# Attention and a squared-ReLU MLP on one core: q and k of four head pairs loaded by rows and turned on TensorE

## The chip, the cores and the metric

One core of one Trainium2 chip runs the kernel. The metric is device time in microseconds, the median of several executions; less is better.

## The reference

```python
# q, k, v: (4, 12, 448, 64) float32; w_in (768, 2048) and w_out (2048, 768), given as 8-byte floats
scores = (q @ k.T) / 8                      # for each of 48 heads, causal mask
attn   = softmax(scores)                    # rows of 448
x      = (attn @ v) -> (1792, 768)          # heads side by side
out    = relu(x @ w_in) ** 2 @ w_out        # float32, (1792, 768)
```

## The kernel before

The 48 heads are worked as 24 pairs. Twelve pairs (`NA = 12`, numbered n = 0 to 11, batches 0 and 1) make up the first stage; the other twelve are spread over the MLP of the first half of the rows. The fifth to the eighth pair are n = 4 to 7. Even pairs use one set of buffers (names beginning with a: `ak`, `aq`, `akt`, `aqt`, `ap`, `apt`), odd pairs another (`bk`, `bq`, ...).

For the scores TensorE wants q and k with the 64 dimensions of each head on the partitions (128 for a pair) and the 448 positions along the free dimension. `load_qk` (L350) gets there in two steps: four DMAs for q and four for k of each pair, each 448 pieces of 128 bytes (32 floats), put 32x32 blocks side by side, and `transposed` (L369) turns the blocks with one VectorE instruction for each of q and k.

A pair then goes: scores on TensorE (L388), row minimum with mask on VectorE (L401), exponential on ScalarE (L405), normalisation on GpSimd or VectorE (L414, L416), 16 TensorE transposes of the probabilities in four groups of four (L428), each group copied out of PSUM by ScalarE or VectorE (L312 or L436), the product with v on TensorE (L448), and two instructions that leave x as a high and a low part (L312, L315).

The weights come as 8-byte floats in pieces of 128 rows (L589, `words`), which ScalarE (twice L312), VectorE (L597, L315, L600) and GpSimd (L325, L319) turn into two 4-byte parts. The first MLP product (L636, L637, L638: three matmuls for each step) fills TensorE between the pairs as soon as x and the weight piece of a step exist; two PSUM banks are set aside for it.

A planner in the kernel sets the order of all work. Each step is given a rank, the engines that could do it with a cost, and what it reads and writes; `emit` places the steps one after the other in a model of the engines' times and writes each engine's instructions in that order. A step with two ways (for instance copying a group out of PSUM on ScalarE or VectorE) gets the one whose modelled end, plus a bias of 0.5 for ScalarE and 1.0 for VectorE, comes first. All DMAs that matter here are issued by SyncE (SP) in one queue, in the planner's order, 0.5 us each in its model. Each engine runs its instructions strictly in order.

PSUM has eight banks; the planner lets up to two at a time hold turned blocks (kind `pt`), four scores, one the product with v, two the MLP.

Of the kernel before, what the change touches and what calls it, by code (L numbers as in the profile page):

```python
# [9 lines left out]
F32 = mybir.dt.float32  # L10
# [7 lines left out]
PE, ACT, DVE, POOL, DMA, DMA2 = range(6)  # L18
# [143 lines left out]
def t_act(n, psum=False, more=0):  # L162
    return n / 1200 + (0.17 if psum else 0.215) + 0.15 * more


def t_dve(n, fast=False):
    return n / 1920 + 0.15 if fast else n / 960 + 0.15
# [13 lines left out]
def t_dma(count, size):  # L181
    return count * (0.0084 + size * 0.0000488) / 16
# [3 lines left out]
def kernel(  # L186
# [17 lines left out]
    nc = tc.nc  # L204
    B, H, S, D = q.shape
    DM = out.shape[1]
    DFF = w_in.shape[1]
    P = 128
    QC = P // 2
    NQ = S // QC  # L210
    NK = -(-S // P)
# [26 lines left out]
    PCW = max(GF * P, CH)  # L238
    NRAW, NZ, NB, NR = 3, 3, 1, 6
    HWAY, OWAY, GWAY = slice(None), slice(1, 2), slice(0, 1)  # L240
    TURNS, LEAD = (0, 3, 2, 1), 15
    CB = NP // 2
    CBW = CB * P
# [17 lines left out]
    plan = Plan()  # L261

    def tiles(nm, n, shape, dtype, pool=const):
        return [pool.tile(shape, dtype, name=f"{nm}{i}") for i in range(n)]

    early = ExitStack()
    pool = early.enter_context(tc.tile_pool(name="early", bufs=1, side="right"))
    ident = pool.tile([P, 3 * QC], F32, name="ident")
# [33 lines left out]
    for i in range(2):  # L302
        m = mask[i * QC:(i + 1) * QC, S - QC:]
        nc.gpsimd.affine_select(
            out=m, in_=m, pattern=[[-1, QC]], base=0,
# [5 lines left out]
    def on_act(n, dst, src, psum=False, func=AF.Copy, more=0, **kw):  # L311
        return (ACT, t_act(n, psum, more), lambda: nc.scalar.activation(dst(), src(), func, **kw))  # L312
# [25 lines left out]
    def attention(s, n, at):  # L338

        b, hp = divmod(n, NP)  # L340
        nm = s.nm
        spare = (lambda us: us) if n >= NA else (lambda us: 0.0)

        def load_qk(key, src, t, j):


            queue, eng = (DMA2, nc.scalar) if n < 2 and key == "q" else (DMA, nc.sync)
            for h in range(D // SQ):
                i = (j * D + h * SQ)
                plan.op(at - 14, [(queue, 0.5, lambda h=h, i=i: eng.dma_start(  # L350
                    out=t[i:i + SQ].rearrange("p (b d) -> p b d", d=SQ),
                    in_=src[b, 2 * hp + j, :, h * SQ:(h + 1) * SQ].rearrange(
                        "(b p) d -> p b d", p=SQ),
                ), t_dma(S, 128))], [], [(nm, key, j, h)])

        def load_v():
# [3 lines left out]
            for kc in range(NK):  # L360
                def go(kc=kc, rows=min(P, S - kc * P)):
# [3 lines left out]
                plan.op(at + V_AT[min(n, 2)] + V_STEP * kc, [(DMA, 0.5, go, t_dma(2 * NV * min(P, S - kc * P), 256))],  # L365
                        [], [(hold, kc)], [taken])

        def transposed(key, src, dst, at):
            plan.op(at, [(DVE, t_dve(S), lambda: nc.vector.transpose(dst, src))],  # L369
                    [(nm, key, j, h) for j in range(2) for h in range(D // SQ)], [(nm, key + "t")])  # L370
# [82 lines left out]
                    [(vr, kc) for kc in range(NK)] + [(nm, "pt", i) for i in range(len(TURNED) // 4)], [av], take=av, drop=[vr],  # L453
                    lag=spare(1.0))

        for j in range(2):
            load_qk("k", k, s.k, j)
        for j in range(2):
            load_qk("q", q, s.q, j)
        if n % NV == 0:  # L460
            load_v()
        vr = vs[n // NV]
        transposed("k", s.k, s.kt, at)
        transposed("q", s.q, s.qt, at + 1)
        at += 4
        groups = (ORDER[:3], ORDER[3:]) if n < NA else (ORDER,)
        for chunks in groups:
# [16 lines left out]
        if n < NA:  # L484
            x = x_t[n]
# [592 lines left out]
    PAIR = 8.6  # L1078
    H_US, O_US = 3 * t_mm(S), 3 * t_mm(CH)
    stack, middle = ExitStack(), ExitStack()  # L1080
    odd = Buffers("b", stack.enter_context(tc.tile_pool(name="b", bufs=1)))
    for n in range(NA):
        attention((even, odd)[n % 2], n, n * PAIR)
    start = NA * PAIR + 4
# [42 lines left out]
    for i, n in enumerate(turns):  # L1127
        attention(even, n, start + i * (rank - start - 42) / NA)
# [76 lines left out]
```

## Time and profile before

| | us |
|---|---|
| median of three runs | 612.62 |
| the three runs | 611.44, 612.62, 615.09 |
| the profiled execution: device time | 611.87 |
| its span, first to last instruction | 610.1 |
| TensorE busy, share of the span | 591.2, 97% |
| VectorE, ScalarE, GpSimd busy | 447.0, 357.6, 350.7 |
| mean granted TensorE clock | 0.996 |

The profiled execution is 0.75 us under the median of the runs; 1.8 us of its time lie outside the span. The busy time of TensorE is partly modelled, since its matmuls are pipelined: a busy stretch may still hold gaps.

### The profile page before, as it was taken

What the parts mean: (1) busy time and instruction counts of PE and PEld (TensorE: products, weight loads), DVE (VectorE), ACT (ScalarE), POOL (GpSimd) and SP (SyncE); (2) the same over time, 40 slices, a digit from 0 to 9 for tenths busy, and PEclk for the clock granted to TensorE, in tenths of its full rate; (3) what the DMA queues carried; (4) which work ended last, traced back from release to release, by engine and by line L of the source; (5) the groups of instructions that cost most, each with busy time, mean ns of one, the idle gap of its engine ahead of it and who ended that gap; (6) DMA issues with size and microseconds to landing.
All of it is one profiled execution on the core that took longest, in us unless ns stands there. A gap on an engine that the chain in (4) does not pass through costs nothing.

```text
span 610.1 us, 11412 instructions
## 1 busy us (share of the span) xinstructions
PE 591.2 (97%) x3718; PEld 510.7 (84%) x3718; DVE 447.0 (73%) x961; ACT 357.6 (59%) x880; POOL 350.7 (57%) x459
## 2 busy tenths in 40 slices
PE   3989999999999999999999999999999999999997
PEld 1656677889988988888898889989989999999996
DVE  4988984476886898674887326769996688779764
ACT  3889997766786745677455542256665743652400
POOL 2465773556669756877744864225894666575100
PEclk9998999999999999999999999999999999999999
DMA  9888973598888998999998477867877847863555
GB/s 143 174 178 143 187 175 57 126 311 275 233 239 264 291 241 222 263 280 269 243 266 283 155 197 221 287 198 199 203 142 175 207 123 145 192 144 64 170 91 91
DMA packets 201788, 120.01 MB, mean 197 GB/s; under 512 B 137152, under 2 KB 189696, under 8 KB 201728
## 3 DMA queue, kind: packets, MB, share of 16 engines
q1 hardware_dynamic: 180624, 107.99, 64.9%
q0 software_dynamic: 6912, 9.44, 10.3%
q10 hardware_dynamic: 14192, 1.85, 1.9%
q8 instruction: 29, 0.48, 0.3%
q14 instruction: 31, 0.25, 0.1%
HBM read 80.71 MB, written 38.54 MB: 195 GB/s over the span
## 4 chain that ended last, share of the span: by engine, by line
PE 84%; DMA 5%; DVE 4%; ACT 3%; issue 1%; SPq 1%; POOL 1%; DVEq 0%; ACTq 0%
PE ps L636 7%; PE ps L1055 7%; PE ps L1057 6%; PE ps L1056 6%; PE ps L448 6%; PE ps L638 6%; PE ps L637 6%; PE ps L388 6%; PE ps L428 6%; PE ps L943 5%; PE ps L945 5%; PE ps L944 5%; PE ps L821 4%; PE ps L819 4%; PE ps L817 4%; DMA words<-in_moe_w_in_dram 1%
## 5 line engine op out<-in xcount | busy, mean ns | idle before, releaser
L414 POOL TENSOR_SCALAR ap<-ap,asm 128x128 f32<-128x128 f32 (+6 forms) x122 | 73.7, 623 | 52.6 <-DVE asm L473 41.9
L312 ACT ACTIVATE words<-words 128x384 f32<-128x384 f32 (+3 forms) x131 | 75.1, 598 | 25.7 <-DVE words L315 9.0
L401 DVE CUSTOM_DVE_ANT_0 ps<-ps,mask 128x448 f32<-128x448 f32 (+6 forms) x168 | 68.6, 444 | 22.9 <-PE ps L388 15.0
L1055 PE MATMUL ps<-wo,g 128*128 128x384 f32 x224 | 77.0, 344 | 0.0
L1057 PE MATMUL ps<-wo,g 128*128 128x384 f32 x224 | 75.1, 335 | 0.0
L1056 PE MATMUL ps<-wo,g 128*128 128x384 f32 x224 | 75.0, 335 | 0.0
L636 PE MATMUL ps<-x,wi 128*128 128x448 f32 x192 | 74.7, 389 | 0.0
L638 PE MATMUL ps<-x,wi 128*128 128x448 f32 x192 | 70.4, 367 | 0.4 <-DVE wi L315 0.4
L637 PE MATMUL ps<-x,wi 128*128 128x448 f32 x192 | 70.2, 366 | 0.0
L405 ACT ACTIVATE ap<-ps,mx 128x448 f32<-128x448 f32 (+6 forms) x126 | 58.8, 483 | 15.6 <-DVE mx L401 15.1
L319 POOL TENSOR_TENSOR wi<-words,wi 128x384 fp32r<-128x384 f32 (+1 forms) x47 | 60.3, 1308 | 8.5 <-ACT wi L312 6.9
L325 POOL TENSOR_SCALAR wi<-words 128x384 fp32r<-128x384 f32 (+1 forms) x46 | 31.3, 682 | 56.4 <-DVE words L600 13.3
L312 ACT ACTIVATE r<-ps 128x448 f32<-128x448 f32 x59 | 32.0, 544 | 43.4 <-PE ps L638 14.8
L817 PE MATMUL ps<-x,wi 128*128 128x448 f32 x153 | 56.3, 368 | 0.0
L821 PE MATMUL ps<-x,wi 128*128 128x448 f32 x153 | 56.0, 366 | 0.0
L819 PE MATMUL ps<-x,wi 128*128 128x448 f32 x153 | 56.0, 366 | 0.0
L943 PE MATMUL ps<-g,wi 128*128 128x448 f32 x150 | 55.0, 367 | 0.3 <-ACT sa L312 0.3
L945 PE MATMUL ps<-g,wi 128*128 128x448 f32 x150 | 54.9, 366 | 0.0
L944 PE MATMUL ps<-g,wi 128*128 128x448 f32 x150 | 54.8, 366 | 0.0
L597 DVE TENSOR_SCALAR words<-words 128x384 int32<-128x384 int32 (+1 forms) x56 | 31.9, 573 | 25.3 <-ACT words L312 19.2
L315 DVE CUSTOM_DVE_ANT_0 words<-words 128x768 uint16<-128x768 uint16 (+1 forms) x56 | 44.2, 789 | 6.7 <-ACT words L312 3.2
L312 ACT ACTIVATE apt<-ps 128x512 f32<-128x512 f32 x71 | 39.2, 605 | 16.7 <-PE ps L428 16.5
(144 smaller groups left out, 1487.3 us busy)
## 6 DMA issues: line engine op xcount, KB each, us to landing
words<-in_moe_w_in_dram SPq DMA_DIRECT2D x24, 512.0 KB, 5.2
words<-in_moe_w_out_dram SPq DMA_DIRECT2D x32, 384.0 KB, 4.3
wo_split<-wo SPq DMA_DIRECT2D x26, 384.0 KB, 4.5
wi<-wo_split SPq DMA_DIRECT2D x21, 384.0 KB, 4.0
wo_whole<-words SPq DMA_DIRECT2D x32, 192.0 KB, 3.9
wi_split<-wi SPq DMA_DIRECT2D x24, 256.0 KB, 3.7
v<-in_v_dram SPq DMA_DIRECT2D x24, 192.0 KB, 4.4
wi_whole<-words SPq DMA_DIRECT2D x18, 256.0 KB, 3.8
```

Of the source, the lines that this page charges most:

```text
L312: return (ACT, t_act(n, psum, more), lambda: nc.scalar.activation(dst(), src(), func, **kw))
L636: nc.tensor.matmul(o, w[:, 0], x[:, 0], start=c == 0, stop=False)
L637: nc.tensor.matmul(o, w[:, 0], x[:, 1], start=False, stop=False)
L638: nc.tensor.matmul(o, w[:, 1], x[:, 0], start=False, stop=c == NP - 1)
L817: nc.tensor.matmul(o, w.t[:, 0, c], x[:, 0], start=begin and c == 0, stop=False, skip_group_check=True)
L819: nc.tensor.matmul(o, w.t[:, 0, c], x[:, 1], start=False, stop=False, skip_group_check=True)
L943: nc.tensor.matmul(o, w.t[:, 0, d], g.t[:, 0], start=start, stop=False, skip_group_check=True)
L944: nc.tensor.matmul(o, w.t[:, 0, d], g.t[:, 1], start=False, stop=False, skip_group_check=True)
L945: nc.tensor.matmul(o, w.t[:, 1, d], g.t[:, 0], start=False, stop=stop, skip_group_check=True)
L1055: nc.tensor.matmul(res(), g[:, 0], w[:, 0], start=f == 0, stop=False)
L1056: nc.tensor.matmul(res(), g[:, 0], w[:, 1], start=False, stop=False)
L1057: nc.tensor.matmul(res(), g[:, 1], w[:, 0], start=False, stop=f == GF - 1)
```

## The change

q and k of pairs 4 to 7 no longer pass through the 32x32 blocks. `load_rows` issues two DMAs for q and two for k, one for each head; partition p gets the four consecutive rows 4p to 4p+3, 256 bytes each, on 112 partitions. `turned_rows` then turns each of q and k with four TensorE transposes (112x128 into 128x112) into one PSUM bank of kind `pt`, and one copy out of PSUM, on ScalarE or VectorE, reads the bank with a step of 112 elements so that the positions come out in order. The rows lie in two new buffers shared by the four pairs in turn, so these loads no longer wait for the readers of `ak`, `aq`, `bk`, `bq`. The other 20 pairs are as they were.

```diff
+    ROWS, RB = range(4, 8), S // NK          # RB = 112, NK = 4
...
+        def load_rows(key, src):
+            t = rows_t[n % len(rows_t)][:, "kq".index(key)]
+            for j in range(2):
+                plan.op(at - 14, [(DMA, 0.5, lambda j=j: nc.sync.dma_start(
+                    out=t.rearrange("p (c x) -> p c x", c=NK)[:, :, j * D:(j + 1) * D],
+                    in_=src[b, 2 * hp + j].rearrange("(p c) d -> p c d", c=NK)),
+                    t_dma(S, 4 * D))], [], [("rows", n % len(rows_t), key, j)])
+
+        def turned_rows(key, dst, at):
+            ps = Hold("ps", "pt")
+            t = rows_t[n % len(rows_t)][:, "kq".index(key)]
+            def go():
+                for c in range(NK):
+                    nc.tensor.transpose(ps.t[:, c * RB:(c + 1) * RB], t[:, c * P:(c + 1) * P], ident[:RB, :RB])
+            def src():
+                return ps.t[:, :S].rearrange("p (c i) -> p i c", c=NK)
+            def to():
+                return dst.rearrange("p (i c) -> p i c", c=NK)
+            plan.op(at, [(PE, NK * 0.109, go)], [("rows", n % len(rows_t), key, j) for j in range(2)], [ps], take=ps, clear=[(nm, key + "t")])
+            plan.op(at, [
+                on_act(S, to, src, True),
+                (DVE, t_dve(S) + 0.05, lambda: nc.vector.tensor_copy(to(), src())),
+            ], [ps], [(nm, key + "t")], drop=[ps])
...
-        for j in range(2):
-            load_qk("k", k, s.k, j)
-        for j in range(2):
-            load_qk("q", q, s.q, j)
+        rows = n in ROWS
+        if rows:
+            load_rows("k", k)
+            load_rows("q", q)
+        else:
+            for j in range(2):
+                load_qk("k", k, s.k, j)
+            for j in range(2):
+                load_qk("q", q, s.q, j)
...
-        transposed("k", s.k, s.kt, at)
-        transposed("q", s.q, s.qt, at + 1)
+        if rows:
+            turned_rows("k", s.kt, at)
+            turned_rows("q", s.qt, at + 1)
+        else:
+            transposed("k", s.k, s.kt, at)
+            transposed("q", s.q, s.qt, at + 1)
...
+    rows_t = tiles("rows", 2, [RB, 2, 2 * NK * D], F32, pool)
```

## Rows read from the trace of the kernel before

**Rows 1.** The page: busy time of TensorE, and TensorE in 40 slices.

```profile
PE 591.2 (97%) x3718; PEld 510.7 (84%) x3718; DVE 447.0 (73%) x961; ACT 357.6 (59%) x880; POOL 350.7 (57%) x459
...
PE   3989999999999999999999999999999999999997
```

**Rows 2.** Stretches: length, busy time (count) by engine, clock, DMA share, GB/s.

```profile
20.62:62.22 41.60, 38.17 (x324) 24.84 (x325) 35.09 (x114) 35.50 (x108) 22.60 (x41) 0.96 0.84 162
...
44.00:50.00 6.00, 5.04 (x34) 2.33 (x36) 3.89 (x14) 5.96 (x19) 2.49 (x5) 0.72 0.96 196
62.22:110.00 47.78, 47.17 (x419) 34.53 (x414) 36.69 (x127) 40.47 (x123) 28.63 (x49) 1.00 0.65 131
```

**Rows 3.** Chain of waits, 16 to 56 us: start, length, what.

```profile
24.58 4.33 DMA words<-in_moe_w_in_dram
...
39.11 4.62 DMA words<-in_moe_w_in_dram
...
44.33 0.58 ACT bpt L312
...
52.48 1.75 PE ps L428 x16
```

**Rows 4.** SyncE's issues in order of time, 19 to 47 us: start, length, what.

```profile
19.22 2.05 SPq L350 DMA_DIRECT2D ak<-in_k_dram  x4
21.37 3.16 SPq L350 DMA_DIRECT2D aq<-in_q_dram  x4
...
33.00 2.87 SPq L350 DMA_DIRECT2D ak<-in_k_dram  x4
35.97 3.04 SPq L350 DMA_DIRECT2D aq<-in_q_dram  x4
...
42.51 3.51 SPq L350 DMA_DIRECT2D bq<-in_q_dram  x4
```

**Rows 5.** Issue times in ns (min/median/max) of two loads, 0 to 110 us, and landing.

```profile
L350 SPq DMA_DIRECT2D bk<-in_k_dram x24: 312/477/1864, 3.3 to 72.8; - x24
...
DMA to landing us min/median/max: 2.1/3.4/5.4
...
L362 SPq DMA_DIRECT2D v<-in_v_dram x20: 379/496/2558, 6.6 to 90.6; - x20
```

**Rows 6.** DMA, 57 to 61 us, only 128-byte packets: packets, and the queue's share.

```profile
DMA packets 2941, 0.36 MB, mean 91 GB/s; under 512 B 2941, under 2 KB 2941, under 8 KB 2941
...
q1 hardware_dynamic: 2941, 0.36, 56.5%
```

**Rows 7.** DMA, 46.6 to 50.9 us, mostly v in 256-byte packets.

```profile
DMA packets 2161, 0.96 MB, mean 224 GB/s; under 512 B 2033, under 2 KB 2033, under 8 KB 2161
...
q1 hardware_dynamic: 2161, 0.96, 97.6%
```

**Rows 8.** TensorE in order of time, 17 to 75 us (idle before, and who ended it).

```profile
40.89 2.25 PE L428 MATMUL ps<-ident,bp 128*128 128x128 f32 x16
44.96 4.01 PE L388 MATMUL ps<-bkt,bqt 64*64 64x448 f32 x28 [1.83 <-ACT bpt L312]
48.90 2.16 PE L448 MATMUL ps<-bpt,v 128*64 128x448 f32 x16
...
54.15 2.23 PE L388 MATMUL ps<-akt,aqt 64*64 64x448 f32 x28
56.31 1.95 PE L448 MATMUL ps<-apt,v 128*64 128x448 f32 x16
```

**Rows 9.** Groups by line and shape, 20.62 to 62.22 us: busy us, mean ns.

```profile
L428 PE MATMUL ps<-ident,bp 128*128 128x128 f32 x48 | 7.2, 279 | 1.1 <-POOL bp L414 0.8
...
L312 ACT ACTIVATE words<-words 128x512 f32<-128x512 f32 x5 | 3.5, 700 | 3.6 <-DMA words<-in_moe_w_in_dram 3.6
...
L312 ACT ACTIVATE x<-ps 128x448 fp32r<-128x448 f32 x5 | 2.8, 554 | 0.8 <-PE ps L448 0.8
...
L369 DVE STREAM_TRANSPOSE akt<-ak 128x448 f32<-128x448 f32 x3 | 1.9, 627 | 0.0
```

**Rows 10.** Groups by line and shape, whole span.

```profile
L312 ACT ACTIVATE apt<-ps 128x512 f32<-128x512 f32 x71 | 39.2, 605 | 16.7 <-PE ps L428 16.5
...
L436 DVE COPY apt<-ps 128x512 f32<-128x512 f32 x1 | 0.7, 650 | 0.0
```

More of the change, by code (lines that the diff above doesn't have):

```diff
@@ L1080 @@
     stack, middle = ExitStack(), ExitStack()
-    odd = Buffers("b", stack.enter_context(tc.tile_pool(name="b", bufs=1)))
+    pool = stack.enter_context(tc.tile_pool(name="b", bufs=1))
+    odd = Buffers("b", pool)
+    rows_t = tiles("rows", 2, [RB, 2, 2 * NK * D], F32, pool)
     for n in range(NA):
```

## The prediction, made before the changed kernel ran

> **What bounds the kernel now.** I read the page first, then busy time in stretches, then the chain of waits and SyncE's queue in the stretch that the change touches. Over the whole span TensorE is the bound: 97% busy, nines in nearly every slice from the third on [rows 1]. So a microsecond of TensorE work added where it is full costs a microsecond, and one of its idle time removed early is gained at the end, since everything behind starts sooner. The change reaches from the loads of pair 4 (19.22 us) to the scores of pair 7 (near 62 us), so I took 20.62 to 62.22, which holds five pairs from one product with v to another.
>
> There TensorE is busy 38.17 of 41.60 us, ScalarE 35.50, VectorE 35.09, and the clock averages 0.96 [rows 2]. So 3.43 us of plain TensorE idle are there to be had. From 62.22 to 110 it is busy 47.17 of 47.78 [rows 2]: little is left.
>
> The chain of waits says why TensorE idles. Twice it passes through SyncE's queue and a load of weights: `words` issued at 24.58 and at 39.11, landing 4.33 and 4.62 us later [rows 3]. ScalarE waits 3.6 us in all for the two [rows 9]. Behind the second wait stand, in ScalarE's order, the copies of turned probabilities (44.33 [rows 3]) that free PSUM banks, so TensorE stops for 1.83 us [rows 8]. Then it runs slow: the granted clock is 0.72 on average from 44 to 50 us [rows 2], between the levels of 2.4 and 1.2 GHz, after an idle time and a burst of transposes; the scores take 4.01 us where the next pair's take 2.23, the product with v 2.16 instead of 1.95 [rows 8]. That is 1.8 + 0.2 = 2.0 us more.
>
> And why were the weights late? Ahead of the `words` at 39.11 stand eight loads of pair 6, issued from 33.00 to 39.01; ahead of that at 24.58, eight of pair 4, from 19.22 to 24.53 [rows 4]. These are the loads that the change replaces.
>
> **The change part by part.**
>
> Loads. Pairs 4 to 7 now take 32 issues. Their eight groups on SyncE, first at 19.22 and last at 42.51, add up to 22.3 us [rows 4], 0.70 each, against a median of 0.48 [rows 5]: the queue is held up. Afterwards there are 16. The nearest row for 448 pieces of 256 bytes is v, whose issue has a median of 0.50 [rows 5]; the bounds are 0.48 and the held-up 0.70. So 16 x 0.50 to 0.70 = 8 to 11 us: SyncE is freed of 11 to 14 us.
>
> The DMA engines gain less. From 57 to 61 us 2941 packets of 128 bytes took 56.5% of 16 engines x 4.0 us = 36.2 us, 12.3 ns each [rows 6]. For 256 bytes the bounds are 12.3 ns (size costs nothing) and 24.6 (size is all). With v, 67.1 us went to 0.96 MB in 2161 packets [rows 7], 0.52 MB of it in 256-byte packets: shared by bytes, 18 ns each, by count 31. I take 22, inside the bounds. Then 32 x 448 = 14,336 packets x 12.3 / 16 = 11.0 us become 7,168 x 22 / 16 = 9.9. So I count on earlier issue, not on a freer network.
>
> What that gives: eight loads took 5.9 us before the second `words`; four take 2.0 to 2.8. It is issued at least 3 us sooner, more than the longer ScalarE wait, and the same holds for the first. So the 3.6 us of ScalarE wait go, with the 1.83 us stop and the 2.0 us of slow clock behind it. The work late next is ScalarE's own.
>
> VectorE loses eight transposes of 0.627 = 5.0 us [rows 9]. Nothing waits for VectorE alone here, so I credit nothing for it; it is room for copies.
>
> TensorE gains 32 transposes. A burst of 16 in the chain took 1.75 us, 0.11 each [rows 3], on 128x128; 112 columns can cost a little less, and 0.11 x 112/128 = 0.096 is the low bound. Bounds 3.1 to 3.5 us; I take 3.5. The high bound is another matter: one instruction lasts 0.279 [rows 9], and if they did not overlap it would be 32 x 0.279 = 8.9.
>
> The Trainium skill speaks against the edit here: "TensorE: Matmul & The Clock Gate", Part 4 (PE-mode transpose), gives about 275 ns for a 128x128 transpose inside a kernel, so 32 would cost 8.8 us by it, 5.3 more than my term. The 279 ns row agrees with it as the length of one instruction; the burst of 16 in 1.75 us says that, as a cost, it does not hold here.
>
> Copies. Eight copies of 448 columns out of PSUM. Nearest is x from PSUM on ScalarE, 0.554 [rows 9]; the step of 112 is not in the trace. The nearest row with a stepped read is `words`, every second word of 512, 0.700, against 0.605 for 512 in a row [rows 9, 10]. Bounds 0.55 to 0.70; I take 0.55, as one element still comes per step. On ScalarE that is 4.4 us, up to 5.6. The two-way choice fell to ScalarE 71 times against once to VectorE in the even pairs' copies [rows 10], so I expect six or more of eight on ScalarE.
>
> Waits added. In TensorE's order the transposes stop everything behind them if rows are late; that shows as a TensorE wait for a DMA. Loads land 3.4 us after issue (median) [rows 5], they go out sooner, and no longer wait for readers of the old buffers, so I cost that at nothing. The cover is SyncE's freed time; without it each late group costs its lateness in full. Each turn also takes one of the two `pt` banks, six times for a pair where it was four; a copy of 0.6 us frees a bank, so that too is hidden unless ScalarE runs late.
>
> **The sum.** Two floors for the 41.60 us stretch. TensorE: 38.17 - 2.0 (clock) + 3.5 = 39.7. ScalarE: 35.50 + 4.4 = 39.9, or 38.8 with two copies on VectorE. Relief in the chain is not the limit: 3.6 + 2.0 = 5.6 would allow 36.0. So the stretch takes about 39.6: a gain of 2.0 us. The profiled execution goes from 611.87 to 609.9; its 0.75 under the median added back, 610.6.
>
> **The rivals.**
>
> *More comes back.* A modelled busy time hides gaps: the burst of 16 transposes at 40.89 takes 2.25 us, not 1.75 [rows 8, 3]. If the new transposes fall into such gaps and VectorE takes half the copies, ScalarE's floor is 35.5 + 2.2 = 37.7 and TensorE's near 38. For it: VectorE has 5 us freed. Against: the choice row above. Then about -4.5 us, 608.1, at best all 5.6, 607.0.
>
> *The wait stays.* The planner draws the whole order anew, and the weights may be held by their own buffers or transfer. TensorE's 3.5 us then fall partly into the idle that stays. About +0.5, 613.
>
> *The other side: TensorE pays in full.* The weights' wait stays as a wait of the in-order engines and all 32 transposes sit where TensorE is full. Price 3.5: 616.1. For it: TensorE floor and ScalarE floor both lie within 2 us of the stretch. It decides as soon as less than 0.4 us of the 5.4 us of idle and slow clock comes back.
>
> *Transposes do not overlap.* Each costs its length: 8.9 instead of 3.5, so 610.6 + 5.4 = 616.0. Against: the burst row. This is the case of the skill's page named above.
>
> *The change does not do what it says*: the piece size is fixed by the rows' 256 bytes and the transposes by the code, so I give this nothing.
>
> **How the numbers follow.** Forecast, 610.6, between 609.2 and 612.3 by its own terms: 0.42. More comes back: 0.27. The wait stays: 0.11. TensorE pays: 0.13. No overlap: 0.04. Another slow clock stretch (2.0 us) on top of a lost gain: 0.03. About 0.5%, 3.1 us, is what a measurement here can tell from none: faster means under 609.6, slower over 615.7. Faster takes the second case and a share of 0.07 of the first: 0.34. Slower: 0.13 + 0.04 + 0.03 = 0.20. Same: 0.46. The range runs from the best case, 607.0, to the dear ones with half a microsecond of margin, 616.5.
>
> **What would show it.** Right: SyncE's L350 issues for pairs 4 to 7 under 11 us in all; no ScalarE wait of 2 us for `words` near 40; clock near 1.00 from 44 to 50; four new transposes in about 0.44 us; copies of 448 near 0.55, most on ScalarE; the end of pair 5's product with v about 2 us earlier. Wrong: a TensorE wait for the row loads, copies near 1 us, or a new stop of TensorE elsewhere before 70 us because the order was redrawn.

## The result, and the profile after

| | before | after |
|---|---|---|
| median, us | 611.81 (8 runs, 611.01 to 615.09) | 617.47 (8 runs, 614.80 to 619.03) |
| ratio, 95% interval | | 1.0076 [1.0055, 1.0097] |
| profiled execution, us | 611.87 | 617.39 |
| its span, us | 610.1 | 615.5 |

The changed kernel is 0.76% slower by the ratio (5.7 us by the medians), 1 us above the end of the predicted range. These are the lines of its page that answer to [rows 1]:

```profile
PE 592.1 (96%) x3750; PEld 513.8 (83%) x3750; DVE 447.1 (73%) x958; ACT 359.2 (58%) x883; POOL 352.8 (57%) x459
...
PE   3997999999999999999999999999999999999997
```

TensorE has 32 instructions more and its busy time is up by 0.9 us; 4.5 of the 5.4 us of span are idle. The third slice rose from 8 to 9, the fourth (46 to 62 us) fell from 9 to 7. Stretches of the changed kernel, with the columns of [rows 2]: ten microseconds of that slice; the five pairs of the 41.60 us there, between the same two products with v; and from there to pair 11's product with v:

```profile
50.00:60.00 10.00, 5.45 (x37) 4.05 (x40) 4.02 (x8) 6.71 (x20) 3.24 (x8) 0.66 0.89 209
...
20.62:66.41 45.79, 39.08 (x356) 28.34 (x356) 33.98 (x111) 37.18 (x113) 23.85 (x42) 0.93 0.74 161
66.41:115.28 48.87, 48.35 (x426) 35.63 (x421) 37.23 (x127) 41.54 (x127) 28.41 (x49) 1.00 0.57 117
```

The stretch of 41.60 us [rows 2] takes 45.79 now: 4.2 us lost here. The next 48.87 us took 49.30 before (62.22 to 111.52): nothing lost there. All engines thin out from 50 to 60 us, where TensorE is busy 5.45 of 10 us at a mean clock of 0.66. TensorE's order of time shows what was won ahead of that and what was lost in it. The lines of the changed kernel have other numbers: L417 are the scores, L434 the exponential, L457 the transposes of probabilities, L477 the product with v, L384 the new transposes.

```profile
42.31 1.91 PE L457 MATMUL ps<-ident,bp 128*128 128x128 f32 x16
44.15 1.91 PE L417 MATMUL ps<-bkt,bqt 64*64 64x448 f32 x28
45.99 1.95 PE L477 MATMUL ps<-bpt,v 128*64 128x448 f32 x16
...
54.65 3.89 PE L457 MATMUL ps<-ident,ap 128*128 128x128 f32 x16 [4.55 <-ACT bp L434]
58.46 2.12 PE L417 MATMUL ps<-akt,aqt 64*64 64x448 f32 x28
60.51 1.95 PE L477 MATMUL ps<-apt,v 128*64 128x448 f32 x16
```

Pair 3's product with v, at 48.90 before [rows 8], begins at 45.99: the old stop of 1.83 us and its slow scores (4.01 us, now 1.91) are gone, a gain of 2.9 us. Pair 4's product, at 56.31 before, begins at 60.51, 4.2 us late: TensorE stops for 4.55 us, and the 16 transposes behind the stop take 3.89 us where those at 42.31 took 1.91. In between 7.1 us were lost, from 2.9 ahead to 4.2 behind. The chain of waits names what TensorE stood for (start, length, what):

```profile
46.55 0.48 SPq L351
...
47.47 0.31 SPq L351
...
47.90 5.06 DMA words<-in_moe_w_in_dram
...
53.54 0.97 ACT bp L434 x4
...
54.65 1.09 PE ps L457 x4
```

and ScalarE's order of time says how long it waited for that load:

```profile
46.59 0.19 ACT L434 ACTIVATION_READ_ACCUMULATOR bp<-ps,mx 128x1 f32 x1
52.98 0.66 ACT L313 ACTIVATE words<-words 128x512 f32<-128x512 f32 x1 [6.20 <-DMA words<-in_moe_w_in_dram]
```

A wait of 6.20 us for weights, where the two of before add up to 3.6 [rows 9]. The load is the fifth of `w_in`, issued at 47.90, when ScalarE had already waited for 1.1 us. It lands 5.06 us later, against 4.62 at 39.11 [rows 3], so the late issue makes the wait and not a slow transfer. In the kernel before it went out with the fourth, at 39.11, ahead of the loads of pairs 8 and 9, the first of which is the last line here:

```profile
39.11 0.90 SPq L589 DMA_DIRECT2D words<-in_moe_w_in_dram  x2
...
46.13 0.41 SPq L589 DMA_DIRECT2D words<-in_moe_w_in_dram  x1
...
50.95 2.34 SPq L350 DMA_DIRECT2D ak<-in_k_dram  x4
```

SyncE's queue in the changed kernel, with the columns of [rows 4], shows what stands ahead of the fifth load now:

```profile
31.92 1.08 SPq L627 DMA_DIRECT2D words<-in_moe_w_in_dram  x2
33.11 1.24 SPq L373 DMA_DIRECT2D rows<-in_k_dram  x2
34.40 4.28 SPq L351 DMA_DIRECT2D ak<-in_k_dram  x4
38.71 2.15 SPq L351 DMA_DIRECT2D aq<-in_q_dram  x2
40.96 1.23 SPq L373 DMA_DIRECT2D rows<-in_q_dram  x2
42.24 1.14 SPq L351 DMA_DIRECT2D aq<-in_q_dram  x2
43.42 2.04 SPq L351 DMA_DIRECT2D bk<-in_k_dram  x4
45.58 2.21 SPq L351 DMA_DIRECT2D bq<-in_q_dram  x4
47.90 1.16 SPq L627 DMA_DIRECT2D words<-in_moe_w_in_dram  x1
```

The third and fourth load of weights go out at 31.92 and 0.54 later, so the fourth, at 39.11 before, is 6.6 us earlier: that is the relief the prediction counted on. But then come 16 loads into `ak`, `aq`, `bk`, `bq`: those of pairs 8 and 9, 11.8 us of issuing. In the kernel before they stand behind the sixth load of weights (46.13), from 50.95 on. Pairs 4 to 7 no longer use these buffers, so they are free once pairs 2 and 3 are turned, and the planner, which counts 0.5 us for an issue, fills the freed queue with them.

### The profile page after: what moved, and what is told of

Same layout as the page of the kernel before. It is cut to its first block, busy times and chain, and to the rows that moved or that the text cites. A ratio compares the mean times of both kernels' runs of the same rounds, so it can differ in the third digit from the quotient of the medians.

```text
span 615.5 us, 11446 instructions
## 1 busy us (share of the span) xinstructions
PE 592.1 (96%) x3750; PEld 513.8 (83%) x3750; DVE 447.1 (73%) x958; ACT 359.2 (58%) x883; POOL 352.8 (57%) x459
## 4 chain that ended last, share of the span: by engine, by line
PE 83%; DVE 6%; DMA 5%; ACT 2%; issue 1%; POOL 1%; SPq 0%; DVEq 0%; ACTq 0%; POOLq 0%
PE ps L674 7%; PE ps L1093 7%; PE ps L457 7%; PE ps L1094 6%; PE ps L1095 6%; PE ps L676 6%; PE ps L675 6%; PE ps L477 6%; PE ps L417 6%; PE ps L981 5%; PE ps L983 5%; PE ps L982 5%; PE ps L857 4%; PE ps L859 4%; PE ps L855 4%; DVE g L316 1%
## 5 line engine op out<-in xcount | busy, mean ns | idle before, releaser
L434 ACT ACTIVATE ap<-ps,mx 128x448 f32<-128x448 f32 (+6 forms) x126 | 58.7, 483 | 16.4 <-DVE mx L430 15.9
L635 DVE TENSOR_SCALAR words<-words 128x384 int32<-128x384 int32 (+1 forms) x56 | 32.1, 575 | 22.7 <-ACT words L313 22.3
```

## The experiments

Two theories at first. Q: the order in SyncE's queue, with the loads of pairs 8 and 9 ahead of weights, makes the loss. T: TensorE pays for the 32 transposes in full. Each ratio is to the kernel before, run beside the variant on the same chip, 30 to 35 runs of it. Its median was 612.64 beside the first four variants below; 612.96 beside the loads behind the sixth, the fifth load alone, half of the change, and earlier rows; and 612.64 beside the rest. Each variant has 9 to 12 runs. Variants are best compared with one another, and with the changed kernel (1.0076), by their ratios. Each trace is of one execution, and its time is given where it lies at the edge of its runs.

### Only SyncE's order: the 16 loads behind the fifth load of weights

The changed kernel; after the planner has set every order, the 16 loads are moved back in SyncE's.

```diff
         order.sort(key=lambda x: x[:2])
+        moved = [x for x in order if x[2].tag in (("qk", 8), ("qk", 9))]
+        order = [x for x in order if x[2].tag not in (("qk", 8), ("qk", 9))]
+        at = next(i for i, x in enumerate(order) if x[2].tag == ("words", "i", 0, 4)) + 1
+        order[at:at] = moved
...
```

> The changed kernel with one move in SyncE's queue: the q and k loads of pairs 8 and 9 go out right behind the fifth weights load instead of ahead of it; the order of all other engines is the changed kernel's. Theory Q (the fifth weights load stands behind loads that the change set free): ScalarE's wait of 6.2 us near 47 to 53 us falls under 1 us, TensorE's stop of 4.55 us and the slow clock behind it go, and the time falls by 5 to 7 us to 610 to 612.5. Theory T (TensorE pays for the 32 transposes): the wait only shifts and the time stays at 616 or more.

Measured 615.73, ratio 1.0065 [1.0043, 1.0086]: no gain over the changed kernel that stands clear of the noise. The number of Q failed, and what T expected, a wait that only shifts, came. The fifth load went out at 38.45 and nobody waited for it. SyncE's queue and ScalarE's order of time, in this kernel:

```profile
38.45 0.55 SPq L631 DMA_DIRECT2D words<-in_moe_w_in_dram  x1
...
53.69 0.55 SPq L631 DMA_DIRECT2D words<-in_moe_w_in_dram  x1
```

```profile
58.41 0.66 ACT L317 ACTIVATE words<-words 128x512 f32<-128x512 f32 x1 [4.98 <-DMA words<-in_moe_w_in_dram]
```

It now waits 4.98 us for the sixth load, issued at 53.69 behind the same 16, and TensorE stops 4.61 us. The wait has moved by one piece of weights.

### The old dependence put back, everything planned anew

The changed kernel, but the loads of pairs 8 and 9 may start only once pairs 6 and 7 are turned, as in the kernel before. No instruction is added.

```diff
-            plan.op(at, [(PE, NK * 0.109, go)], [("rows", n % len(rows_t), key, j) for j in range(2)], [ps], take=ps, clear=[(nm, key + "t")])
+            plan.op(at, [(PE, NK * 0.109, go)], [("rows", n % len(rows_t), key, j) for j in range(2)]
+                    + [(nm, key, j, h) for j in range(2) for h in range(D // SQ)], [ps], take=ps, clear=[(nm, key + "t")])
```

> The changed kernel, but the planner lets the q and k loads of pairs 8 and 9 start only after pairs 6 and 7 have been turned, as their buffers demanded before the change. The planner draws its order anew. Theory Q: the fifth weights load goes out ahead of those loads again, near 35 us, and the time is 608 to 612. Theory T: 615 or more.

Measured 610.76, ratio 0.9975 [0.9958, 0.9993]: 1.0% under the changed kernel by the ratios, 6.7 us by the medians, with the same loads, transposes and copies. The whole order is another one, so this run alone does not name the part of it that counts; the reverse test below does. Its SyncE queue, and the longest of TensorE's waits in it:

```profile
35.30 0.55 SPq L628 DMA_DIRECT2D words<-in_moe_w_in_dram  x1
...
38.88 3.64 SPq L351 DMA_DIRECT2D ak<-in_k_dram  x4
...
48.01 0.67 SPq L628 DMA_DIRECT2D words<-in_moe_w_in_dram  x1
48.74 2.73 SPq L351 DMA_DIRECT2D bk<-in_k_dram  x4
```

```profile
24.67 0.57 PE L384 MATMUL ps<-ident,rows 112*128 112x112 f32 x4 [0.69 <-DMA rows<-in_q_dram]
...
32.35 0.57 PE L384 MATMUL ps<-ident,rows 112*128 112x112 f32 x4 [1.76 <-DMA rows<-in_k_dram]
```

The fifth load is out at 35.30 and ScalarE waits for no weights. What TensorE waits for now is rows, 2.45 us in these two, which the prediction had costed at nothing.

### The 32 transposes alone

The kernel before, in its own order; two groups of four transposes of probabilities in each of pairs 4 to 7 are done twice. These have 128 columns, not 112.

```diff
+            twice = 4 <= n < 8 and i < 2
...
-                for n, (c, kc) in enumerate(blocks):
+                for _ in range(1 + twice):
+                    for m, (c, kc) in enumerate(blocks):
...
```

> The kernel before, in its own order, with 32 TensorE transposes more: in pairs 4 to 7 the first two of the four groups of turned probabilities are turned twice into the same bank. Nothing else differs. Theory T: TensorE is full, so the time rises by 3.1 to 3.5 us, to about 616. Theory Q: the transposes fall largely into idle time of 30 to 62 us, and the time rises by 0.5 to 2 us.

Measured 615.49, ratio 1.0041 [1.0021, 1.0061]: 2.5 us by the ratio, of 3.5 us of transposes. It lies between the theories' numbers; most of the work is paid where nothing else changes. The profiled execution (613.52, the second lowest of twelve) is no plain measure of it: TensorE's stop is there, 2.13 us, but the stretch behind it keeps its clock:

```profile
44.00:50.00 6.00, 4.78 (x45) 2.58 (x46) 4.26 (x19) 5.99 (x19) 2.68 (x6) 1.00 0.92 179
```

### The loads alone

The kernel before, in its own order: in place of the 32 loads of pairs 4 to 7 the 16 loads by rows, which nobody reads. The four pairs are computed from the q and k of pairs 2 and 3, still in the buffers.

```diff
+            def row(h):
+                if h == 0:
+                    nc.sync.dma_start(
+                        out=rows_t[n % 2][:, "kq".index(key)].rearrange("p (c x) -> p c x", c=NK)[:, :, j * D:(j + 1) * D],
+                        in_=src[b, 2 * hp + j].rearrange("(p c) d -> p c d", c=NK))
...
-                plan.op(at - 14, [(queue, 0.5, lambda h=h, i=i: eng.dma_start(
+                plan.op(at - 14, [(queue, 0.5, lambda h=h, i=i: row(h) if 4 <= n < 8 else eng.dma_start(
...
```

> The kernel before, in its own order, with the 32 loads of q and k of pairs 4 to 7 replaced by 16 loads by rows into tiles that nobody reads; those pairs compute with the q and k of pairs 2 and 3 still in the buffers, so four pairs of the output are not the reference's. It measures the relief of SyncE's queue alone. Theory Q: the fourth and fifth weights loads go out 3 us sooner, ScalarE's waits of 0.8 and 2.7 us and the slow clock go, and the time falls by 2 to 4 us. Rival N (the DMA engines are the limit, and 256-byte pieces are no cheaper): weights land no sooner, and the time is within 1 us of before.

Measured 609.50, ratio 0.9952 [0.9934, 0.9970]: -3.1 us by the medians, -2.9 by the ratio. The waits for weights on ScalarE are down to 0.2 us, in a profiled execution of 611.63, the slowest of its twelve. The relief of SyncE is real when the order of the queue stays, and rival N of the expectation, under 1 us, is out.

### The 16 loads behind the sixth, and behind the seventh load of weights

As the first experiment, with another place:

```diff
-        at = next(i for i, x in enumerate(order) if x[2].tag == ("words", "i", 0, 4)) + 1
+        at = next(i for i, x in enumerate(order) if x[2].tag == ("words", "i", 0, 5)) + 1
...
+        at = next(i for i, x in enumerate(order) if x[2].tag == ("words", "o", 0, 0)) + 1
```

> The changed kernel with the q and k loads of pairs 8 and 9 put behind the sixth weights load in SyncE's queue (one load further than in the run that put them behind the fifth); the order of all other engines is the changed kernel's. Theory Q (weights loads stand behind loads set free by the change; behind the fifth alone, the wait moved to the sixth): both waits are gone, and the time is 609 to 612. Theory T (TensorE pays for the transposes): 615 or more.

> The changed kernel with the q and k loads of pairs 8 and 9 behind the seventh weights load in SyncE's queue; all other engines keep the changed kernel's order. Behind the fifth and the sixth, the ScalarE wait had moved to the next weights load each time (6.2, then 5.0, then 4.4 us). Theory Q (the loads of pairs 8 and 9 ahead of weights are the cause): no weights wait over 2 us is left, and the time is 609.5 to 612.5. If ScalarE's order simply asks for weights sooner than SyncE can issue them, a wait of 2 to 4 us appears at some load again and the time is 613 to 616.

Behind the sixth: 615.63, ratio 1.0043 [1.0022, 1.0063]. The number of Q failed again. ScalarE waits for the seventh load, issued at 54.24 (this profiled execution, 612.49, is among the fastest of its twelve):

```profile
57.50 0.54 ACT L317 ACTIVATE words<-words 128x384 f32<-128x384 f32 x1 [4.43 <-DMA words<-in_moe_w_out_dram]
```

Behind the seventh: 613.55, ratio 1.0009 [0.9993, 1.0025]. No wait for weights over 1.02 us is left, as Q said, and most of the loss is gone, but the time is a microsecond above Q's range. The moved loads are now late themselves: VectorE waits 1.00 us for `aq` at 57 us. ScalarE then waits 2.76 us for GpSimd's `bp` before 70.21 and TensorE behind it:

```profile
71.29 0.97 PE L421 MATMUL ps<-akt,aqt 64*64 64x256 f32 x12 [1.65 <-ACT apt L317]
```

So moving loads under orders that were made for another queue passed the wait on here, to the next piece of weights and then to other engines. The last step is read from the trace alone; nothing was tried on it.

### The reverse: the good kernel with the bad place

The kernel with the old dependence; only SyncE's order is changed, the 16 loads moved ahead of the fifth load of weights.

```diff
+        moved = [x for x in order if x[2].tag in (("qk", 8), ("qk", 9))]
+        order = [x for x in order if x[2].tag not in (("qk", 8), ("qk", 9))]
+        at = next(i for i, x in enumerate(order) if x[2].tag == ("words", "i", 0, 4))
+        order[at:at] = moved
...
```

> The reverse: the kernel that holds back pairs 8 and 9 (610.8 us), with the 16 loads of those pairs moved ahead of the fifth weights load in SyncE's queue, as they stand in the changed kernel; all other engines keep their order, and the result stays the reference's. Theory Q: ScalarE waits 4 to 6 us for the fifth weights load, TensorE stops and runs slow behind it, and the time rises to 614 to 618. If the queue's order is not the cause: 610 to 612.

Measured 616.70, ratio 1.0061 [1.0040, 1.0082]: 0.86% lost by that move alone, 5.3 us by the ratios and 5.9 by the medians, as Q said. SyncE, ScalarE and TensorE of this kernel (its profiled execution, 614.10, is the fastest of nine):

```profile
35.31 4.20 SPq L355 DMA_DIRECT2D ak<-in_k_dram  x4
39.55 2.72 SPq L355 DMA_DIRECT2D aq<-in_q_dram  x4
42.32 2.05 SPq L355 DMA_DIRECT2D bk<-in_k_dram  x4
44.46 1.99 SPq L355 DMA_DIRECT2D bq<-in_q_dram  x4
46.57 0.40 SPq L632 DMA_DIRECT2D words<-in_moe_w_in_dram  x1
```

```profile
50.84 0.66 ACT L317 ACTIVATE words<-words 128x512 f32<-128x512 f32 x1 [4.20 <-DMA words<-in_moe_w_in_dram]
```

```profile
52.16 1.01 PE L388 MATMUL ps<-ident,rows 112*128 112x112 f32 x4 [3.19 <-ACT bp L439]
```

The same picture as in the changed kernel: 16 issues, then the weights, then the stop.

### The fifth load alone moved late

The kernel with the old dependence; in SyncE's order the fifth load of weights is moved behind the loads of pair 8.

```diff
+        late = next(x for x in order if x[2].tag == ("words", "i", 0, 4))
+        order.remove(late)
+        at = max(i for i, x in enumerate(order) if x[2].tag == ("qk", 8)) + 1
+        order.insert(at, late)
...
```

> The kernel that holds back pairs 8 and 9 (610.8 us), with one move in SyncE's queue: the fifth weights load goes out behind the loads of pair 8, next to the sixth; all other engines keep their order. The reverse test. Theory Q: the ScalarE wait for the weights comes back with 4 to 6 us, with a TensorE stop and a slow clock behind it, and the time rises by 4 to 7 us to 615 to 618. If the place of this load in the queue is not the cause, it stays within 1 us of 610.8.

Measured 611.25, ratio 0.9976 [0.9959, 0.9992], no change from 610.76. As a test it failed: in the program the load now stands behind its first reader, which therefore takes the words that are there and waits for nothing (that piece of weights is worked out from older words). It says nothing on Q; the reverse test above takes its place.

### The late loads not made at all

The changed kernel without the fifth to the seventh load of weights; those pieces are worked out from the words that lie in the buffers.

```diff
+        there = (kind, gr, a, ch) in (("i", 0, 4, 0), ("i", 0, 5, 0), ("o", 0, 0, 0))
-        plan.op(rank - 12, [(DMA, 0.5, lambda: nc.sync.dma_start(out=raw.t[:, :n], in_=src), t_dma(P, 8 * n))],
+        plan.op(rank - 12, [(DMA, 0.5, lambda: there or nc.sync.dma_start(out=raw.t[:, :n], in_=src), t_dma(P, 8 * n))],
```

> The changed kernel without its fifth, sixth and seventh weights loads (those three pieces are worked out from words that earlier loads left in the buffers, so parts of the output are not the reference's); all orders are the changed kernel's. ScalarE has nothing to wait for there. Theory Q: the 6.2 us wait, the 4.55 us stop and the slow clock go, and the time falls by 5 to 7 us to 610 to 612. Theory T (transposes and copies are the price): it stays at 615 or more.

Measured 610.74, ratio 0.9961 [0.9940, 0.9981]: 6.7 us under the changed kernel, with its 16 loads as early and every other order unchanged. The waits for these pieces hold the whole loss and more; three loads less are also three issues and their bytes less, which this run does not tell apart. TensorE still waits for rows (1.20 us at 25.18, and this):

```profile
31.93 0.57 PE L384 MATMUL ps<-ident,rows 112*128 112x112 f32 x4 [1.32 <-DMA rows<-in_k_dram]
```

### Half of the change, earlier rows, and dearer issues in the plan

Three tries for a better version. Pairs 4 and 5 only, with the old dependence (`ROWS = range(4, 6)`); the old dependence with pair 5's loads of rows ahead of the last three of four loads of v; and the changed kernel with the planner told 0.66, 0.6 and 0.8 us for an issue of rows, of q and k, and of v.

```diff
-    ROWS, RB = range(4, 8), S // NK
+    ROWS, RB = range(4, 6), S // NK
...
```

> The change for pairs 4 and 5 only, with the loads of pairs 6 and 7 held until the turn of pairs 4 and 5. Half the transposes and copies, and SyncE's relief where the first late weights load stood. If the place of the weights loads decides and TensorE pays about 0.8 us for each pair turned, 609 to 612; if the order drawn anew puts a weights load late again, 614 or more.

```diff
+        late = [x for x in order if x[2].tag and x[2].tag[:2] == ("v", 1) and x[2].tag[2] > 0]
+        order = [x for x in order if x not in late]
+        at = max(i for i, x in enumerate(order) if x[2].tag == ("rows", 5)) + 1
+        order[at:at] = late
...
```

> The kernel that holds back pairs 8 and 9, with the row loads of pair 5 put ahead of the last three v loads in SyncE's queue; all other engines keep their order. There TensorE waited 1.8 and 0.7 us for row loads. If that wait costs what it shows, it goes and the time falls by 1 to 2 us to 609 to 610; if other engines were as late, nothing changes.

```diff
...
-                plan.op(at - 14, [(DMA, 0.5, lambda j=j: nc.sync.dma_start(
+                plan.op(at - 14, [(DMA, 0.66, lambda j=j: nc.sync.dma_start(
```

> The changed kernel with the planner told what the trace shows of SyncE's issues: 0.66 us for a row load, 0.6 for a 128-byte load of q or k, 0.8 for v, in place of 0.5. It draws its order anew. If the waits come from an order that believes SyncE faster than it is, they shrink and the time is 609 to 613; if the order only shifts the late load, 614 to 618.

Half: 614.26, ratio 1.0015 [0.9995, 1.0036]. ScalarE waits for weights again, 1.61 us near 39 and 2.16 us near 59: with half of the relief the weights are late again.

Rows first: 611.24, ratio 0.9973 [0.9956, 0.9989], no better than 0.9975 without it. The wait for rows is gone, and TensorE stands for ScalarE near the same places:

```profile
25.05 0.57 PE L388 MATMUL ps<-ident,rows 112*128 112x112 f32 x4 [1.11 <-ACT ap L439]
35.05 1.09 PE L462 MATMUL ps<-ident,ap 128*128 128x128 f32 x8 [1.05 <-ACT apt L317]
```

Dearer issues: 614.75, ratio 1.0026 [1.0007, 1.0046]: half a per cent under the changed kernel, in the range that was given for a load that is only shifted. But ScalarE waits for no weights; the new order loses elsewhere, as the stretches show:

```profile
20.00:30.00 10.00, 7.15 (x60) 4.88 (x53) 7.37 (x25) 8.32 (x27) 3.98 (x9) 0.80 0.82 181
30.00:40.00 10.00, 9.37 (x79) 7.01 (x78) 6.20 (x19) 7.22 (x20) 5.44 (x8) 0.86 0.99 212
```

TensorE waits 1.84 us for rows there, and 1.01 us for VectorE's part in a piece of weights.

## Why the prediction was wrong

**What failed.** The step under *Waits added*: the row loads "no longer wait for readers of the old buffers, so I cost that at nothing". It looked at the loads that leave the buffers and not at those that come into them next. Freeing `ak` to `bq` lets the loads of pairs 8 and 9 start 16.5 us earlier, 34.40 against 50.95, past two loads of weights in SyncE's queue; their 16 issues, 11.8 us there, were never counted, and they take all that SyncE was freed of (22.3 us of issuing became 11.1). With it fell "so the 3.6 us of ScalarE wait go": they went, and 6.20 us came. Put back, the old dependence gives 610.76; the bad place alone, in that kernel, gives 616.70; the loads of weights taken out give 610.74. That is shown from both sides. The sign that the prediction named for being wrong, a new stop of TensorE before 70 us because the order was redrawn, is what came.

**The relief of SyncE** was sized well. The 16 loads by rows take 11.1 us of issuing, the upper end of 8 to 11; the second load of weights goes out 2.4 us earlier (22.15), short of the 3 us that the prediction called the least, the fourth 6.6; the first stop and its slow clock are gone at 45.99. The loads alone gave 2.9 to 3.1 us.

**TensorE's term** was near. Groups of the changed kernel from 15 to 70 us, by line and shape:

```profile
L384 PE MATMUL ps<-ident,rows 112*128 112x112 f32 x32 | 4.3, 266 | 1.3 <-ACT ap L434 1.1
...
L394 DVE COPY bqt<-ps 128x448 f32<-128x448 f32 x2 | 1.2, 600 | 0.9 <-PE ps L384 0.9
...
L313 ACT ACTIVATE akt<-ps 128x448 f32<-128x448 f32 x2 | 1.1, 534 | 0.0
```

and a piece of its chain of waits:

```profile
36.22 0.39 PE ps L384 x4
```

One transpose lasts 266 ns, and four take 0.39 us in the chain (0.57 at 25.15, right behind a stop), so 32 in a full stretch take 3.1 us, the low bound. Paid in the time of the kernel, the 32 transposes done twice cost 2.5 us. The rival in which they do not overlap is refuted: 266 ns is the length of one, 98 ns what each adds. The Trainium skill, "TensorE: Matmul & The Clock Gate", Part 4 (PE-mode transpose), gives about 275 ns for 128x128 in bf16; as a length the 266 ns agree with it, as a cost it does not hold here.

**Copies.** 534 to 583 ns on ScalarE, as taken; the step of 112 columns costs nothing that shows. But four of eight went to VectorE (600 to 617 ns), not two at most.

**Row loads.** Costed at nothing; once the weights are on time they cost TensorE 2.45 us of waiting. Removing that wait gained nothing that shows (ratio 0.9973 against 0.9975): ScalarE was late by about a microsecond at two places near by.

**The sum** of -2.0 us is met in size by the change with the old dependence (-1.9 us by the medians, -1.5 by the ratio), but in part by luck. The parts measured alone, -2.9 us for the loads and +2.5 for the transposes, leave -0.4. Nor does the gain lie where it was forecast, in the stretch up to pair 5's product with v. That begins in this kernel at

```profile
62.14 1.95 PE L478 MATMUL ps<-bpt,v 128*64 128x448 f32 x16
```

against 62.22 before, with 16 of the pair's scores (about 0.9 us) now ahead of it: a gain of 1.0 us there and not 2.0. At pair 11's product it is 0.5 us (111.05 against 111.52), and of the 1.5 us by which the span is shorter the rest comes behind that. Why was not tried.

**The rivals.** *The wait stays* named the planner's new order and gave it +0.5 us: right place, price too low by 5 us, since it had the old idle time stay and no new wait come. *TensorE pays in full*, 616.1, came nearest in time for another reason: transposes alone cost 2.5 us, and with the order held the kernel is still faster than before.

**Open.** At 115 us the changed kernel is 3.8 us behind (pair 11's product with v, 115.28 against 111.52); the span differs by 5.4. From 400 to 450 us TensorE is idle 1.45 us, against 0.31 in the kernel before; other kernels of this study range there from 0 to 0.95 us. What decides that was not tried.

## What to carry to other kernels

When an edit frees a buffer, ask what will be loaded into it next, and when: in an in-order issue queue an early load that nobody needs yet stands in front of a late one that somebody does. If a planner sets the order, count the edit's effect on every load it may move, and hold loads back by a dependence when the queue is the scarce thing. Judge an order by planning anew with the limit in place; moving one queue's entries under the other engines' old orders only passed the wait on here.

## What the runs showed of the hardware

The time that SyncE takes to issue one load is not fixed: loads of `ak` took 1.07 us each at 34.40 (4.28 for four), where the same shape has a median of 0.48 [rows 5]; a load of rows, with pieces of 256 bytes, had a median of 0.62 us, not the 0.50 of v. What decides it was not tried.

Stops of TensorE of like length did not lower its clock alike, in one execution each. Behind 1.83 us the granted clock was 0.72 on average from 44 to 50 us [rows 2]; behind 2.13 us at the same place, in the kernel with transposes done twice, it was 1.00; why was not tried. In the changed kernel, behind 4.55 us, it was 0.50, the level of 1.2 GHz, from 54.65 to 58.50, and the 16 transposes there took 3.89 us, twice the 1.91 of 16 at 42.31; from 60.5 on it was 1.00.
